# Linear attention and a gated feed-forward: another layout of pieces, tiles, banks and engines

## The chip, the cores and the metric

The kernel runs on one core of a Trainium2 chip. The metric is the device time of one execution in microseconds (us), as a median over runs. The engines are TensorE (PE; PEld is its weight load), VectorE (DVE), ScalarE (ACT) and GpSimd (POOL). SyncE (SP) issues most transfers; they run on the core's 16 DMA engines. Matmuls write to PSUM, which has eight banks, and DVE or ACT copies from there to SBUF.

## The reference

First an attention with a decaying state, per batch b (4) and head h (8), over 768 tokens with head size 48:

```
cur   = (u * k_t) outer v_t
y_t   = r_t . (state + cur)
state = w * state + k_t outer v_t
```

Then the heads are put side by side (x, 768 tokens of 384 channels) and go through a gated linear unit:

```
gate_pre[t] = sum over j of conv_w[j] * x[t - 4 + j]      (5 taps, causal, per channel)
out = (sigmoid(gate_pre) * (x @ w_val)) @ w_out
```

Inputs and outputs are float32; matmul operands are bf16 in both kernels.

## The kernel before

The sequence of each batch is cut in units of W = 256 tokens (12 in all, n = 0 to 11), and a unit in two chunks of 128 (cl, or c). The recurrence is computed by chunks. r and k are scaled by powers of w (dr, dk), transposed by products with an identity, and multiplied to scores; a triangular mask turns the scores into the attention inside a chunk (at); the state z carries what came before the chunk; the bonus u comes in through a row sum s and dv = s * v.

One unit passes through these steps (names in the order string, line of the profile in brackets):

- RS (L245) and KS (L274) scale r and k into rs and ks, on POOL, in some cases on DVE. RT (L259) and KT (L297) transpose them on PE into a bank, eight products of 128 columns each. RE (L267) and KE (L307) copy the banks to rT and kT on ACT. r is loaded with two neighbouring tokens in a partition, so RE undoes that order with a strided write.
- PR (L316) multiplies the transposed k with rT on DVE; S (L328) sums that with u * w on PE; SE (L340) copies the sums on DVE; DV (L343) makes dv on POOL. CV (L283) casts v to vb on ACT.
- A (L357) makes the scores in two banks per chunk, M (L370) masks a bank on DVE. KV (L384) makes the chunk's state on PE, ID (L396) adds the state before on DVE, in PSUM, and ZE (L401) multiplies it with a block mask or the decay, on DVE, to z.
- YD (L412) and Y (L426) gather the output of a chunk in one bank: 3 products with dv, 12 with z, 16 with at. Each of the latter fills a 128x32 tile of the array. YE (L455) copies the bank to xT on ACT.

The feed-forward works on the same 256 tokens. C (L470) is the convolution: per tap a diagonal 64x64 block times xT, 40 products of 256 columns for two thirds of the channels and 40 of 128 for the last third, whose tokens are split over two banks. SG (L483) is the sigmoid on ACT, V (L490, L499) the product with w_val, HT (L512) the product of both on DVE, O (L522) the product with w_out per chunk, OE (L534) the copy on ACT, and st (L538) stores a whole unit, 384 KB. The last unit is done by chunks of 128 (lines 560 to 640).

At the start w is loaded into all 128 partitions by a broadcast transfer (192 KB), its logarithm is taken (LN), and dr and dk follow as exponentials on ACT. Three products on the identity (D, L149) stand in the early PE stream.

There are no loops that set the order: a long string ORDER names every step, and each engine executes its steps in the order of the string. An engine's instruction that waits holds back all that stand behind it on this engine. That goes for SP's transfers too: nearly all loads and all stores but one are in one queue, loads first, and the 11 stores of whole units behind the last load:

```
v:11.1 ... st:4 ... st:0 ... st:1 ... st:2 ... st:7
```

PSUM tiles come from a pool of eight banks in turn; k_st and v_st have seven buffers, r_st six.

Of the kernel before, what the change touches and what calls it, by code (L numbers as in the profile page):

```python
# [12 lines left out]
AX = mybir.AxisListType  # L13
# [3 lines left out]
def kernel(  # L17
# [12 lines left out]
    nc = tc.nc  # L30

    B, H, S, D = r.shape
    C = 128
    NP = H // 2
# [4 lines left out]
    U = 2  # L39
    W = U * C  # L40
    NU = S // W
    N = B * NU

    consts = ctx.enter_context(tc.tile_pool(name="consts", bufs=1))
    persist = ctx.enter_context(tc.tile_pool(name="persist", bufs=1))
    ld = ctx.enter_context(tc.tile_pool(name="ld", bufs=7))
    ldr = ctx.enter_context(tc.tile_pool(name="ldr", bufs=6))
    wk = ctx.enter_context(tc.tile_pool(name="wk", bufs=2))
    atp = ctx.enter_context(tc.tile_pool(name="atp", bufs=4))
    ffn = ctx.enter_context(tc.tile_pool(name="ffn", bufs=2))  # L50
    outp = ctx.enter_context(tc.tile_pool(name="outp", bufs=11))

    psum = ctx.enter_context(tc.tile_pool(name="psum", bufs=8, space=bass.MemoryType.PSUM))

# [3 lines left out]
    def bank(shape=(128, 512), dtype=F32):  # L58
        return psum.tile(list(shape), dtype, name="bank")

    k_st, v_st, r_st = {}, {}, {}

    def load_kv(n, cl, nm, eng):
        b, cu = divmod(n, NU)
        src, d = (k, k_st) if nm == "k" else (v, v_st)
        if n not in d:
            d[n] = ld.tile([128, U, H, D], F32, name=f"{nm}_st")
        t0 = cu * W + cl * C
        eng.dma_start(out=d[n][:, cl], in_=src[b, :, t0 : t0 + C, :].transpose([1, 0, 2]))

    def load_r(n, eng, hs=(0, H)):
        b, cu = divmod(n, NU)
        if n not in r_st:
            r_st[n] = ldr.tile([128, H, 2, D], F32, name="r_st")
        hs = slice(*hs)
        eng.dma_start(
            out=r_st[n][:, hs].rearrange("p h s d -> p h (s d)"),
            in_=r[b, hs, cu * W : cu * W + W, :].rearrange("h (p s) d -> p h (s d)", s=2),
        )

    w_bc = consts.tile([128, H, D], F32)
    cw5 = consts.tile([KW, DM], F32)

    def load_w():
        nc.sync.dma_start(
            out=w_bc.rearrange("p h d -> p (h d)"),
            in_=w.rearrange("(o h) d -> o (h d)", o=1).to_broadcast([128, DM]),
        )

    def load_cw():  # L90
        nc.sync.dma_start(out=cw5, in_=moe_conv_w)

    ident = consts.tile([128, 128], BF16)
    make_identity(nc, ident)
    wt = consts.tile([128, NP], F32)
    nc.vector.memset(wt, 1.0)
    ut = consts.tile([128, NP], F32)
    nc.vector.memset(ut, 0.0)
    nc.scalar.preload_act_table_set("natural_log_exp_and_others")
    for dst, src in ((wt, w), (ut, u)):  # L100
        for par in range(2):
            nc.scalar.dma_start(
                out=dst[64 * par : 64 * par + D, :],
                in_=src.rearrange("(p two) d -> two d p", two=2)[par],
            )


    io_i32 = consts.tile([128, 1], mybir.dt.int32)
    nc.gpsimd.iota(io_i32, pattern=[[0, 1]], base=0, channel_multiplier=1)
    io_j = consts.tile([128, 2], mybir.dt.int32)  # L110
    nc.gpsimd.iota(io_j, pattern=[[1, 2]], base=0, channel_multiplier=2)
    mask = consts.tile([128, 128], BF16)
    make_upper_triangular(nc, mask, val=1.0, diag=False)

    io_f = consts.tile([128, 1], F32)
    nc.vector.tensor_copy(io_f, io_i32)
    sc_k = consts.tile([128, U], F32)
    for cl in range(U):
        nc.vector.tensor_scalar(
            sc_k[:, cl : cl + 1], io_f, scalar1=-1.0, scalar2=float(C - 1 - cl * C),  # L120
            op0=ALU.mult, op1=ALU.add,
        )
    sc_r = consts.tile([128, 2], F32)
    nc.vector.tensor_copy(sc_r, io_j)
    nc.vector.tensor_scalar_add(sc_r, sc_r, float(-C))

    lnw_bc = consts.tile([128, H, D], F32)
    dk = consts.tile([128, U, H, D], F32)
    dr = consts.tile([128, H, 2, D], F32)

    def log_w():
        nc.scalar.activation(out=lnw_bc, in_=w_bc, func=AF.Ln)

    def decay_r():
        for j in range(2):
            nc.scalar.activation(
                out=dr[:, :, j, :], in_=lnw_bc, func=AF.Exp, scale=sc_r[:, j : j + 1]
            )

    def decay_k():  # L140
        for cl in range(U):
            nc.scalar.activation(
                out=dk[:, cl], in_=lnw_bc, func=AF.Exp, scale=sc_k[:, cl : cl + 1]
            )

    def dummy():
        t_ = bank()
        for _ in range(3):
            nc.tensor.matmul(  # L149
                out=t_.rearrange("p (a x) -> p a x", x=128),  # L150
                lhsT=ident,
                rhs=ident[:, None, :].to_broadcast([128, 4, 128]),
                start=True,
                stop=True,
            )

    def ring(name, shape, n, dtype=BF16):
        return [persist.tile(shape, dtype, name=f"{name}{i}") for i in range(n)]

    def heads(t_, n):  # L160

        return t_[:, 16 : 16 + 64 * n].rearrange("p (h x) -> p h x", x=64)[:, :, 0:D]

    def gaps(t_):
        return t_.rearrange("p (h x) -> p h x", x=64)[:, :, 0:16]

    ks_t = ring("ks", [128, U, NP, 2, 64], 3)
    rs_t = ring("rs", [128, 2, NP, 2, 64], 2)
    vb_t = ring("vb", [128, U, H * 64 + 64], 4)
    dv_t = ring("dv", [128, U, DM], 2)  # L170
    xT_t = ring("xT", [128, NT, PAD + S], 2)
    for t_ in rs_t:
        nc.gpsimd.memset(t_[:, :, :, :, D:64].rearrange("p s n a x -> p (s n a) x"), 0.0)
    for t_ in ks_t:
        nc.gpsimd.memset(t_[:, :, :, :, D:64].rearrange("p c n a x -> p (c n a) x"), 0.0)
    for t_ in vb_t:
        nc.gpsimd.memset(gaps(t_.rearrange("p c x -> p (c x)")), 0.0)
    for t_ in xT_t:
        nc.gpsimd.memset(t_[:, :, 0:PAD], 0.0)

    uw2 = consts.tile([128, NP, 2], BF16)
    nc.gpsimd.memset(uw2, 0.0)
    wcm = consts.tile([128, NP, 2, D], F32)
    nc.gpsimd.memset(wcm, 0.0)
    bdm = consts.tile([128, NP, 2, D], F32)
    nc.gpsimd.memset(bdm, 0.0)
    for par in range(2):
        nc.gpsimd.memset(bdm[64 * par : 64 * par + 64, :, par, :], 1.0)

    wv_st = consts.tile([128, NT, DM], F32)
    wo_st = consts.tile([128, NT, DM], F32)

    wval = consts.tile([128, NT, 4, 128], BF16)
    wout = consts.tile([128, 4, DM], BF16)
    cw5b = consts.tile([KW, DM], BF16)
    cwT = consts.tile([128, NT, KW], F32)
    cwd = consts.tile([128, NT, KW, 64], BF16)
    id64 = consts.tile([128, 64], BF16)  # L200

    for q in range(2):
        rows = slice(64 * q, 64 * q + 64)
        nc.vector.tensor_copy(id64[rows], ident[rows, rows])

    def cw_cast():
        nc.vector.tensor_copy(cw5b, cw5)  # L207

    def cw_transp():
        st["cw_ps"] = bank([128, NT, 8], BF16)  # L210
        for T in range(NT):
            nc.tensor.transpose(
                st["cw_ps"][:, T, 0:KW], cw5b[:, T * 128 : T * 128 + 128], ident[0:KW, 0:KW]
            )

    def cw_evac():
        nc.vector.tensor_copy(cwT, st["cw_ps"][:, :, 0:KW])

    def cw_diag():
        nc.vector.tensor_tensor(  # L220
            out=cwd.rearrange("p t k x -> p (t k) x"),
            in0=id64[:, None, :].to_broadcast([128, NT * KW, 64]),
            in1=cwT.rearrange("p t k -> p (t k)")[:, :, None].to_broadcast([128, NT * KW, 64]),
            op=ALU.mult,
        )

    def cast_wval():
        wv = wv_st.rearrange("p k (t x) -> p k t x", x=128)
        nc.gpsimd.tensor_copy(wval[:, :, 0::2, :], wv[:, :, 0::2, :])
        nc.gpsimd.tensor_copy(wval[:, :, 1::2, 64:128], wv[:, :, 1:3, 0:64])  # L230
        nc.gpsimd.tensor_copy(wval[:, :, 1::2, 0:64], wv[:, :, 1:3, 64:128])

    def cast_wout(part):
        if part:
            nc.scalar.copy(out=wout[64:128, 1::2, :], in_=wo_st[0:64, 1:3, :])
            nc.scalar.copy(out=wout[0:64, 1::2, :], in_=wo_st[64:128, 1:3, :])
        else:
            nc.gpsimd.tensor_copy(wout[:, 0::2, :], wo_st[:, 0::2, :])


    st = {}

# [571 lines left out]
```

## Time and profile before

| quantity | value |
|---|---|
| median of 3 runs | 104.72 us (104.08 to 104.97) |
| span of the profiled execution | 102.6 us |
| instructions in it | 4615 |
| moved by DMA | 20.55 MB, 15.54 read from and 4.72 written to HBM |
| DMA packets | 67645, of which 63525 are under 512 B |
| mean granted TensorE clock | 0.944 (0.5 from some 17 to 27 us) |

The span is one execution, from the first to the last instruction on the core; the 2.1 us between it and the median lie around it. A line of the table of groups names a source line, engine, operation and tiles, the busy time, the mean duration and the idle time ahead of it. A line of a stretch gives for each engine its busy time in that stretch and the number of its instructions. The DMA share is the sum of the packets' times over 16 engines; as packets overlap, it can pass 1. Busy PE time is modelled from a pipelined engine, and isn't PE at its peak.

### The profile page before, as it was taken

What the parts mean: (1) busy time and instruction counts of PE and PEld (TensorE: products, weight loads), DVE (VectorE), ACT (ScalarE), POOL (GpSimd) and SP (SyncE); (2) the same over time, 40 slices, a digit from 0 to 9 for tenths busy, and PEclk for the clock granted to TensorE, in tenths of its full rate; (3) what the DMA queues carried; (4) which work ended last, traced back from release to release, by engine and by line L of the source; (5) the groups of instructions that cost most, each with busy time, mean ns of one, the idle gap of its engine ahead of it and who ended that gap; (6) DMA issues with size and microseconds to landing.
All of it is one profiled execution on the core that took longest, in us unless ns stands there. A gap on an engine that the chain in (4) does not pass through costs nothing.

```text
span 102.6 us, 4615 instructions
## 1 busy us (share of the span) xinstructions
PE 84.6 (82%) x2016; PEld 68.3 (67%) x2016; DVE 75.7 (74%) x148; ACT 72.8 (71%) x123; POOL 58.2 (57%) x63
## 2 busy tenths in 40 slices
PE   0002846999987999999899979999899999999980
PEld 0002435878766887898687648997698978887830
DVE  4004465886999998998789499999875986997230
ACT  5056555941988799977969967988798499835840
POOL 7951049799683706983995678738166990140000
PEclk9999996555899999999999999999999999999997
DMA  1799999999888799697979799879899897088673
GB/s 35 145 246 245 207 166 183 237 224 318 151 257 155 150 234 201 125 240 151 255 134 244 151 194 279 163 152 257 123 200 162 163 356 262 6 296 312 233 273 126
DMA packets 67645, 20.55 MB, mean 200 GB/s; under 512 B 63525, under 2 KB 67626, under 8 KB 67626
## 3 DMA queue, kind: packets, MB, share of 16 engines
q1 hardware_dynamic: 65610, 19.77, 86.8%
q10 hardware_dynamic: 2016, 0.49, 2.4%
q8 instruction: 15, 0.25, 1.0%
q14 instruction: 4, 0.03, 0.1%
HBM read 15.54 MB, written 4.72 MB: 198 GB/s over the span
## 4 chain that ended last, share of the span: by engine, by line
PE 51%; DMA 16%; DVE 13%; ACT 8%; issue 4%; POOL 3%; SPq 2%; DVEq 0%; POOLq 0%; ACTq 0%
PE bank L470 8%; PE bank L522 7%; PE bank L426 6%; DMA r_st<-in_r_dram 6%; DMA k_st<-in_k_dram 6%; PE bank L490 5%; DVE at L370 5%; DMA cw<-in_moe_conv_w_dram 5%; PE bank L297 5%; ACT kT L307 4%; PE bank L357 4%; PE bank L259 4%; PE bank L499 3%; PE bank L412 2%; PE bank L384 2%
## 5 line engine op out<-in xcount | busy, mean ns | idle before, releaser
L370 DVE TENSOR_TENSOR at<-bank,mask 128x512 bf16<-128x512 f32 x48 | 31.2, 681 | 3.3 <-PE bank L357 2.9
L343 POOL TENSOR_TENSOR dv<-v_st,s_sb 128x768 bf16<-128x768 f32 x12 | 17.7, 1475 | 12.5 <-DVE s_sb L340 10.9
L274 POOL TENSOR_TENSOR ks<-k_st,dk 128x768 bf16<-128x768 f32 x9 | 16.7, 1859 | 11.8 <-DVE cw5b L207 5.4
L307 ACT COPY kT<-bank 128x1024 bf16<-128x1024 bf16 (+1 forms) x13 | 12.4, 956 | 9.3 <-DVE pr L316 6.4
L267 ACT COPY rT<-bank 128x1024 bf16<-128x1024 bf16 (+1 forms) x13 | 16.1, 1237 | 2.5 <-PE bank L259 2.2
L259 PE MATMUL bank<-ident,rs 128*128 128x128 bf16 x96 | 8.4, 234 | 10.5 <-DVE rs L245 9.7
L245 POOL TENSOR_TENSOR rs<-r_st,dr 128x768 bf16<-128x768 f32 x8 | 14.5, 1818 | 3.0 <-DMA r_st<-in_r_dram 3.0
L522 PE MATMUL bank<-wout,hT 128*128 128x384 bf16 x66 | 14.2, 326 | 0.1
L259 PEld LDWEIGHTS <-rs 128*128 128x128 bf16 x96 | 6.3, 104 | 11.7 <-POOL uw L689 9.7
L455 ACT CAST xT<-bank 128x384 bf16<-128x384 f32 x24 | 10.7, 488 | 4.5 <-PE bank L426 4.4
L512 DVE TENSOR_TENSOR hT<-bank,gate 128x384 bf16<-128x384 f32 x22 | 11.6, 546 | 0.2 <-PE bank L522 0.2
L483 ACT ACTIVATE gate<-bank 128x384 bf16<-128x384 f32 x22 | 9.8, 500 | 2.6 <-PE bank L470 1.8
L470 PE MATMUL bank<-xT,cwd 64*64 64x128 bf16 (+1 forms) x440 | 11.2, 244 | 0.6 <-DVE at L370 0.3
L534 ACT COPY o_sb<-bank 128x384 f32<-128x384 f32 x22 | 10.3, 488 | 1.4 <-PE bank L522 0.9
L470 PEld LDWEIGHTS <-cwd 64*64 64x64 bf16 x440 | 9.7, 106 | 1.9 <-issue 0.8
L490 PE MATMUL bank<-xT,wval 128*128 128x256 bf16 x66 | 10.8, 272 | 0.0
L297 PE MATMUL bank<-ident,ks 128*128 128x128 bf16 x96 | 8.6, 239 | 2.4 <-DVE ks L274 1.4
L316 DVE TENSOR_TENSOR pr<-bank,rT 128x1024 bf16<-128x1024 bf16 (+1 forms) x13 | 8.3, 642 | 3.0 <-ACT kT L307 1.7
L283 ACT CAST vb<-v_st 128x768 bf16<-128x768 f32 x12 | 10.2, 852 | 0.0
L426 PE MATMUL bank<-at,vb 128*32 128x128 bf16 x384 | 9.8, 230 | 0.0
L357 PE MATMUL bank<-rT,kT 48*128 48x128 bf16 x192 | 8.8, 229 | 0.7 <-DVE bank L396 0.3
L297 PEld LDWEIGHTS <-ks 128*128 128x128 bf16 x96 | 6.6, 107 | 4.2 <-DVE ks L274 2.2
(79 smaller groups left out, 140.1 us busy)
## 6 DMA issues: line engine op xcount, KB each, us to landing
k_st<-in_k_dram SPq DMA_DIRECT2D x24, 192.0 KB, 5.4
v_st<-in_v_dram SPq DMA_DIRECT2D x24, 192.0 KB, 4.8
out_dram<-o_sb SPq DMA_DIRECT2D x11, 384.0 KB, 4.5
r_st<-in_r_dram SPq DMA_DIRECT2D x10, 384.0 KB, 5.4
wv_st<-in_moe_w_val_dram SPq DMA_DIRECT2D x1, 576.0 KB, 6.5
wo_st<-in_moe_w_out_dram SPq DMA_DIRECT2D x1, 576.0 KB, 6.3
r_st<-in_r_dram SPq DMA_DIRECT2D x2, 192.0 KB, 5.5
r_st<-in_r_dram ACTq DMA_DIRECT2D x1, 384.0 KB, 5.5
```

What stands on the lines that cost most here:

```text
L245: eng.tensor_tensor(out=rs_t[n % 2][:, :, ps[0] : ps[1], :, 0:D].rearrange("p s n a d -> p (n a) s d"), in0=r_st[n][:, hs], in1=dr[:, hs], ...
L259: nc.tensor.transpose(tr[:, s, p, :], rs_t[n % 2][:, s, ps[0] + p].rearrange("p a x -> p (a x)"), ident,)
L267: nc.scalar.copy(out=st["rT", n][:, ps[0] : ps[1], :].rearrange("x n (i s) -> x s n i", s=2), in_=st["r_tr", n, ps[0]],)
L274: eng.tensor_tensor(out=ks_t[n % 3][:, cs, :, :, 0:D].rearrange("p c n a d -> p c (n a) d"), in0=k_st[n][:, cs], in1=dk[:, cs], op=ALU.mult,)
L297: nc.tensor.transpose(tr[:, c, p, :], ks[:, cls[0] + c, p].rearrange("p a x -> p (a x)"), ident,)
L307: nc.scalar.copy(out=st["kT", n].rearrange("x n (c i) -> x c n i", c=U)[:, cls[0] : cls[1]], in_=tr,)
L343: eng.tensor_tensor(out=dv_t[n % 2].rearrange("p c (h d) -> p (c h) d", d=D), in0=v_st[n].rearrange("p c h d -> p (c h) d"), in1=st["s", n ...
L370: nc.vector.tensor_tensor(out=st["at", n, cl][:, par], in0=st["at_ps", n, cl][par], in1=mask[:, None, :].to_broadcast([128, NP, 128]), op= ...
L426: nc.tensor.matmul(out=y_ps[32 * q : 32 * q + 32, T, :], lhsT=lt, rhs=rh, start=False, stop=last, skip_group_check=True,)
L470: nc.tensor.matmul(out=g_ps[i][64 * qo : 64 * qo + 64, o0 : o0 + n0], lhsT=cwd[rows, T, t, :], rhs=xT[rows, T, t0 + c0 + t : t0 + c0 + t + ...
L490: nc.tensor.matmul(out=v_ps[:, 0:W], lhsT=wval[:, kt, i, :], rhs=xT[:, kt, t0 : t0 + W], start=(kt == 0), stop=(kt == NT - 1), skip_group_ ...
L522: nc.tensor.matmul(out=o_ps, lhsT=hT[:, i, c0 : c0 + C], rhs=wout[:, k, :], start=(j == 0), stop=(j == 2),)
```

## The change

The kernel is written anew, with the same mathematics, 12 units and two chunks. These parts differ:

- The feed-forward has pieces of its own: 384 tokens, half a batch, independent of the units. The last half is cut in 128 and 256.
- The convolution uses 32x32 diagonal blocks: 4 row strips times 3 channel groups, per tap 12 products that each have the whole piece's tokens as columns, and write to three banks. Group T lands rotated by T strips; columns of w_val and rows of w_out are rotated alike, w_out by its transfers (five of them).
- w is loaded as one row of 1.5 KB and spread to 128 partitions by a product with ones (WS, a float32 matmul).
- The copy of the transposed r reads the bank with a stride and writes rT densely; before, it read densely and wrote with a stride.
- The state before is added by a product with the identity on PE (ZI) instead of an addition on DVE (ID).
- PSUM is one tile of eight banks. Each step in ORDER names its bank (@) and, where there is a choice, its engine (/V, /A, /P for DVE, ACT, POOL). Of the 13 copies RE, 6 are on DVE (two of them halves); of the 13 KE, 4; of the 12 SE, 5. POOL has three whole casts of v and a half one, DVE one dv and one xT copy. DVE has one r product and one k product whole and a half of each (before, three whole r, two whole k and two halves of each); POOL has the others.
- No dummy product is named. Rings k_st and v_st have six buffers, the output ring has 12 of 128 tokens.
- A store is 128 tokens (192 KB), 24 in all. Three of them stand in SP's queue ahead of the last load of k, four more ahead of the last load of v.

The core of it, with the lines of the new order that hold the last loads:

```diff
-        for T0, t1, tn in ((0, 0, W), (2, 0, 0)):
-            for t in range(KW):
-                for q in range(2):
-                    for i in range(2):
-                        rows = slice(64 * q, 64 * q + 64)
-                        qo = (q + i) % 2
+    PIECES = (
+        (0, 0, 3), (0, 3, 3), (1, 0, 3), (1, 3, 3), (2, 0, 3), (2, 3, 3),
+        (3, 0, 3), (3, 3, 1), (3, 4, 2),
+    )
+    def conv(m, b):
+        bb, q0, nq = PIECES[m]
+        N, t0 = nq * C, q0 * C
+        for t in range(KW):
+            for q in range(4):
+                for T in range(NT):
+                    rows = slice(32 * q, 32 * q + 32)
+                    qo = (q + T) % 4
+                    nc.tensor.matmul(
+                        out=PS[32 * qo : 32 * qo + 32, b[T], 0:N],
+                        lhsT=cwd[rows, T, t, :],
+                        rhs=xT_t[bb % 2][rows, T, t0 + t : t0 + t + N],
...
-            in_=w.rearrange("(o h) d -> o (h d)", o=1).to_broadcast([128, DM]),
+        q.dma_start(out=wrow, in_=w.rearrange("(o h) d -> o (h d)", o=1))
+    def w_spread(b):
+        nc.tensor.matmul(out=bank(b, DM), lhsT=ones, rhs=wrow, start=True, stop=True)
...
-            out=st["rT", n][:, ps[0] : ps[1], :].rearrange("x n (i s) -> x s n i", s=2),
-            in_=st["r_tr", n, ps[0]],
+            rT_t[n % NRT][:, cut(half, NP)].rearrange("x n (p s) -> x n p s", s=2),
+            bank16(b)[:, cut(half, 1024)].rearrange("x (n s p) -> x n p s", s=2, p=128),
...
-        nc.vector.tensor_tensor(out=kv_ps, in0=kv_ps, in1=st["zin", n, cl], op=ALU.add)
+        nc.tensor.matmul(
+            out=bank(b, DM),
+            lhsT=ident,
+            rhs=z_t[2 * n % NZ].rearrange("p n a d -> p (n a d)"),
+            start=False,
...
+        st:1.1/S st:0.2/S v:11.1/S st:3.2/S O:5.1@0 st:1.2/S v:11.0/S st:3.1/S st:2.1/S st:2.0/S ZE:10.0@1
```

More of the change, by code (lines that the diff above doesn't have):

```diff
@@ L71, in load_r, with bank @@
[L71 to L77, printed above, removed]
+    psum = ctx.enter_context(tc.tile_pool(name="psum", bufs=1, space=bass.MemoryType.PSUM))
+    ctx.enter_context(tc.manual_schedule())
+    PS = psum.tile([128, 8, 512], F32, name="PS")
+    def bank(i, n=512):
+        return PS[:, i, 0:n]
@@ L109 @@
[L109 to L121, printed above, removed]
-        )
@@ L123 @@
[L123 to L137, printed above, removed]
-            )
@@ new lines, in bonus, with evac_s @@
+    def bonus(n, b):
+        for c in range(2):
+            for i in range(NP):
+                nc.tensor.matmul(
+                    out=bank(b)[:, c * H + 2 * i : c * H + 2 * i + 2],
+                    lhsT=pr_t[n % NPR][:, c, i, :],
+                    rhs=uw2[:, i, :],
+                    start=(c == 0 and i == 0),
+                    stop=(c == 1 and i == NP - 1),
+                    skip_group_check=True,
+                )
+    def evac_s(eng, n, b):
+        copy(eng, s_t[n % NDV].rearrange("p s h -> p (s h)"), bank(b, 2 * H))
@@ new lines, in attn @@
+    def attn(n, c, b):
+        rT, kT = rT_t[n % NRT], kT_t[n % NKT]
+        for i in range(NP):
+            for a in range(2):
+                rows = slice(64 * a, 64 * a + D)
+                nc.tensor.matmul(
+                    out=bank(b[a])[:, 128 * i : 128 * i + 128],
+                    lhsT=kT[rows, c, i, :],
+                    rhs=rT[rows, i, C * c : C * c + C],
+                    start=(i == 0),
+                    stop=(i == NP - 1),
+                    skip_group_check=True,
+                )
@@ L151, in dummy, with evac_o, store @@
+    def evac_o(eng, m, i, b):
+        copy(eng, o_t[o_index(m, i) % NO], bank(b, DM))
+    def store(m, i, q):
+        bb, q0, nq = PIECES[m]
+        t0 = (q0 + i) * C
+        q.dma_start(out=out[bb, t0 : t0 + C, :], in_=o_t[o_index(m, i) % NO])
+    def dummy(b):
+        for _ in range(2):
+            nc.tensor.matmul(
+                out=bank(b).rearrange("p (a x) -> p a x", x=128),
                 lhsT=ident,
@@ L171 @@
[L171 to L182, printed above, removed]
```

1046 lines of the change are left out of this document (464 added, 582 removed).

## The prediction

> **What bounds the kernel now.** I read the engines' shares first, then the stretches, then the queue of SP, and the chain of waits last.
>
> The first part of the page:
>
> ```profile
> PE 84.6 (82%) x2016; PEld 68.3 (67%) x2016; DVE 75.7 (74%) x148; ACT 72.8 (71%) x123; POOL 58.2 (57%) x63
> ```
>
> PE has most work, but no engine fills the span. The stretches (span time, length, then PE, PEld, DVE, ACT and POOL busy, the granted clock, the DMA share, GB/s):
>
> ```profile
> 0.00:16.00 16.00, 3.96 (x35) 2.51 (x35) 5.80 (x18) 7.83 (x13) 7.86 (x31) 1.00 0.94 174
> 16.00:36.00 20.00, 18.80 (x405) 15.45 (x409) 17.32 (x31) 13.75 (x20) 15.20 (x12) 0.74 0.97 210
> 36.00:60.00 24.00, 22.90 (x566) 18.61 (x555) 20.80 (x40) 21.54 (x38) 16.62 (x10) 1.00 0.97 193
> 60.00:80.00 20.00, 19.42 (x523) 16.48 (x522) 17.45 (x34) 15.65 (x27) 12.57 (x8) 1.00 0.97 189
> 80.00:92.00 12.00, 12.00 (x311) 10.02 (x313) 10.62 (x21) 9.16 (x16) 5.94 (x4) 1.00 0.70 223
> ```
>
> From 16 to 80 us two resources are full at once: PE (18.8 of 20, 22.9 of 24, 19.4 of 20) and the DMA engines, at 0.97 throughout. The rate is only 190 to 210 GB/s there; the page counts 63525 of 67645 packets under 512 B. The timeline of SP says the same (start, length, line, transfer):
>
> ```profile
> 0.75 0.43 SPq L69 DMA_DIRECT2D k_st<-in_k_dram  x1
> ...
> 49.13 3.33 SPq L69 DMA_DIRECT2D v_st<-in_v_dram  x2
> ...
> 76.14 0.71 SPq L69 DMA_DIRECT2D k_st<-in_k_dram  x1
> 76.89 2.94 SPq L69 DMA_DIRECT2D v_st<-in_v_dram  x2
> 80.33 17.84 SPq L538 DMA_DIRECT2D out_dram<-o_sb  x11
> ```
>
> An issue into an empty queue takes 0.43 us. The 49 issues from 16.72 to 79.83 take 61.0 of those 63 us, 1.2 each: SP is held up by the transfers ahead of it. The last k is issued at 76.14, and POOL's last key product starts on it at 81.21. After the last loads all stores follow, up to the end. The chain of waits (start, length, piece) is PE nearly alone from 74 us:
>
> ```profile
> 75.56 1.80 PE bank L470 x80
> ...
> 88.59 0.90 PE bank L426 x56
> ...
> 95.67 1.00 PE bank L560 x80
> ```
>
> So before, loads and PE run neck and neck to 80 us, and PE with a backlog sets the end. The execution profiled has a span of 102.6 us; the median of the runs is 104.72, so 2.1 us lie around the span, and I add them to each span below.
>
> **The change, part by part.** *Convolution on PE.* Now 80 products of a 256-token unit take 1.79 us (80 in 1.80 above): 11 units 19.7 us, the last one (L560) 1.0, together 20.7. They go away. Instead 540 products of 32x32 come in nine pieces of 60. No 32x32 product is in the trace. Low end: 12.5 ns each, as L560 goes (80 in 1.00); high end: no more side by side than the 64x64 ones, 15,360 columns in 1.79 us, so 23,040 columns of a 384-token piece take 2.7. I take the 128x32 products of L426, which are short and packed (56 in 0.90, 16 ns each): 0.96 a full piece, 0.75 for the two short ones, 8.2 in all. Bounds 6.8 and 21.5.
>
> The Trainium skill ("TensorE: Matmul & The Clock Gate", section "Measured speedup vs the span model") measured 6.32 times the speed of one tile for nine 32x32 tiles and 10.6 for sixteen. Twelve are in turn here; about 8 would be 1.2 us a piece, an estimate from that page, and the sum below would be 2 us larger. The rows for column tiles here (56 in 0.90, 3.3 side by side of four) are of the same kind.
>
> *Other PE work.* The carry moves from DVE into 8 identity products of 384 columns: 8 x 0.163 (three L522 take 0.49) = 1.3. The three dummies (1.5) go. Spreading w is one fp32 product of 384 columns; the trace has no fp32 product, so between 0.16 and four times a half-clock 0.33; I take 0.6. Values and projections have as many columns as before. PE: 84.6 - 20.7 - 1.5 + 8.2 + 1.3 + 0.6 = **72.5** (71 to 86).
>
> *DVE.* Off: four r and k products by shapes 2.8 + 2.0, the carry 8 x 0.558 = 4.5, half the diagonals 0.85, seven s copies 1.2. On: one dv 1.1, one xT copy 0.55, the memsets of vb (between 0.06 and 0.33 each) 0.8, small ones 0.1, four kT copies, and four and two halves of rT. A kT copy is dense bf16 from a bank, as pr (0.684) is: 2.7. The rT copy reads with a stride of 128 elements, not in the trace. Low end 0.68; high end the dearest rate of DVE, k's product (768 in 1.483), so 1.98. I take 1.2, the one-per-cycle rate of the mask rows (384 in 0.55, 512 in 0.68), as a stride spoils pairing at worst: 4 x 1.2 + 2 x 0.68 = 6.2. DVE: 75.7 - 11.35 + 11.45 = **75.8** (73 to 82): no relief.
>
> *ACT.* rT: 16.1 becomes 7 x 1.02 (the dense kT row; 1.33 if the strided side costs alike on the read) = 7.2; kT 12.4 becomes 8.3; casts of v 10.2 become 7.3; seven s copies +1.4; weights -0.8. 72.8 becomes **57.5** (up to 60). *POOL.* One and a half more k and two and a half more r products (1.86, 1.82) +7.4, casts of v +2.9, one dv -1.5, weights -1.8, memsets -1.2: 58.2 becomes **64**.
>
> *Transfers.* r, k, v and the output move the same bytes in the same packets. Only w's broadcast (192 KB) goes; w_out comes in five parts, stores in 24 of 192 KB, not 11 of 384. Six k and v buffers instead of seven cost nothing: a buffer's products are done some five units before its turn. The queue is full, so what is moved counts by place: three stores now stand ahead of the last k and four more ahead of the last v. A 192 KB store is 0.63 us at the 313 GB/s of the 92 to 96 us stretch, a 192 KB load 1.04 at 189. Each of these stores waits on SP for its copy by ACT, and every load behind it waits too; the three belong to the first two pieces, whose copies stand by the scores of units 4 and 5 in the order, and the loads behind them are of units 9 to 11, so I cost the wait at nothing (an ACT copy late by x moves the end by x). The last k: 81.2 - 0.6 (w) + 3 x 0.63 + 0.5 (an estimate for the start, where all of r goes by SP and none by ACT) = 83.0. The last v: + 4 x 0.63 + 2 x 1.04 = 87.6.
>
> *From there.* v cast 0.82, dv 1.48 (POOL): 89.9. y products 0.34 + 0.90, xT 0.55: 91.7. Convolution 0.75, three gates 1.2, hT 0.42, two projections 0.98, copy 0.49: 95.6. Store 1.9 to land, 1.0 to the end as before (issue 99.88, 1.7 to land, span 102.6): 98.5. By the queue alone, 17 stores after the last v: 87.6 + 10.7 + 1.0 = 99.3. The road over k (83.0, 1.82, transposes 0.45, copy and pr 1.4, scores 0.56, four masks 2.7) is at 89.9, no later. I take a span of 99.0: **101.1 us**. PE's 13 us mostly turn into waiting for loads: 10 units at 7.0 us of DMA against 6.0 of PE and 6.2 of DVE.
>
> **Rivals.** *Transfers go faster once fewer things stand beside them.* For: 260 GB/s from 20 to 24 us; against: 0.97 in every stretch, at rates that don't follow PE. Then DVE's 6.3 a unit sets the pace: the second unit's keys at 14, ten units 77, 16 us of tail and stores: 93 to 94, about **96 us**. *32x32 products run only as many at once as 64x64 ones.* PE is 86 again, starts some 1 us earlier, with its old idle 18: about 103, **105 us**, no change.
>
> *Slower: evacuation becomes the bound.* DVE keeps 75.8 us of work, now with strided copies between PE's products and the scores (RE and KE at L250). Its idle time, 102.6 - 75.7 = 26.9, need not shrink: if it is start, end and turns with PE, each us of DVE work is one of span. At strided copies near 1.7, halfway to the high end, DVE is 78; with k copies at 1.2, 80: 107 span, **108 us**. It decides above a DVE sum of about 77. For: DVE is full at 87% from 16 to 92 us. Against: among the waits PE's own for DVE are small after the start (the scores wait 0.3 us for it), while DVE waits 2.9 us for the scores. The Trainium skill ("TensorEngine Tiling (Array Packing)", section "PSUM Bottleneck") says this too: a tiled TensorE may leave the copies out of PSUM as the bottleneck. The trace agrees so far that PE waits little for them before.
>
> **How the numbers follow.** Forecast 0.48, faster transfers 0.13, no packing 0.13, evacuation 0.26. The first two lie below 103.7, the last above 105.8: faster by over 1% 0.61, within 1% (about what a measurement of this kernel can tell) 0.13, slower 0.26. The range runs from 97.5, inside the second case, to 107, inside the last, and leaves out some 0.2. The likeliest sign's own range is 98 to 103.7.
>
> **What would show it.** PE near 72 us busy with gaps in mid-kernel; a convolution piece near 0.96; DMA still at 0.95 or more up to some 85 us; SP's issues still over 1 us; the last k product near 83; ACT under 61, DVE near 76. Wrong if loads end well before 80 us, if DVE's sum passes 78, or if PE waits mostly for DVE and ACT rather than for products of loaded data.

## The result, and the profile after

The changed kernel took 98.70 us in the median of 6 runs (98.12 to 101.70); the kernel before took 104.30 beside it (6 runs, 103.33 to 104.97). The ratio is 0.947, with a 95% interval of 0.941 to 0.953. Some executions of one kernel take a few per cent longer than the rest: times here are medians of all runs, ratios are taken over the faster runs alone, and the execution whose profile is read (100.07 us, span 98.1, where most had spans of 96.2 to 96.8) is one of the longer.

The page of the changed kernel: the engines' shares, then the queue that SP and ACT fill, then the shares of the chain of waits.

```profile
PE 84.0 (86%) x1962; PEld 61.1 (62%) x1962; DVE 78.0 (80%) x145; ACT 59.0 (60%) x117; POOL 64.5 (66%) x69
...
q1 hardware_dynamic: 66748, 20.07, 85.2%
...
PE 50%; DVE 17%; POOL 12%; DMA 7%; issue 6%; ACT 3%; SPq 1%; POOLq 0%; DVEq 0%
```

ACT lost 13.8 us, POOL gained 6.3, DVE 2.3. PE's busy time hardly fell (84.6 before); its weight loads did (68.3 before). The queue's share, last in its line, is the time of all its packets over 16 engines: 85.2% of 98.1 us is 83.6 us an engine. Before, it was 86.8% of 102.6, 89.1 us, for nearly the same bytes.

The stretches of the changed kernel (span time, length, PE, PEld, DVE, ACT and POOL busy, granted clock, DMA share, GB/s):

```profile
0.00:16.00 16.00, 7.80 (x76) 5.82 (x77) 10.79 (x28) 8.99 (x14) 10.27 (x30) 1.00 0.93 195
16.00:36.00 20.00, 18.90 (x446) 13.70 (x445) 16.75 (x29) 12.14 (x23) 17.34 (x17) 1.00 0.95 221
36.00:60.00 24.00, 23.68 (x530) 16.91 (x525) 22.20 (x38) 15.77 (x33) 17.79 (x12) 1.00 0.98 211
60.00:80.00 20.00, 19.00 (x521) 14.35 (x520) 17.25 (x30) 13.84 (x28) 16.31 (x11) 1.00 0.90 212
80.00:92.00 12.00, 12.00 (x388) 8.85 (x387) 9.93 (x20) 5.61 (x16) 2.80 (x3) 1.00 0.64 226
```

The DMA engines are about as full as before, but move 195, 221, 211 and 212 GB/s where they moved 174, 210, 193 and 189. That is this execution: in another profile of the same kernel (the third group below) it was 217, 181 and 201 GB/s from 16 to 80 us, with the DMA engines at 0.93, 0.86 and 0.90. PE does 7.8 us of work in the first 16 us (3.96 before). As its busy time is only 0.6 us less in the whole, 3.9 of the 4.5 us that the span lost are idle time of PE, and nearly all of that lies before 16 us.

SP's timeline of the changed kernel (start, length, line, transfer), at its last loads:

```profile
72.33 2.09 SPq L268 DMA_DIRECT2D k_st<-in_k_dram  x2
74.53 1.52 SPq L538 DMA_DIRECT2D out_dram<-o  x2
76.15 0.40 SPq L268 DMA_DIRECT2D v_st<-in_v_dram  x1
76.64 1.11 SPq L538 DMA_DIRECT2D out_dram<-o  x2
77.81 0.46 SPq L268 DMA_DIRECT2D v_st<-in_v_dram  x1
78.32 17.24 SPq L538 DMA_DIRECT2D out_dram<-o  x17
```

The last k is issued at 73.72 and has landed at 77.2 (before: 76.14 and 80.9), although three stores now stand ahead of it. The last v has landed at 82.0 (before: 83.7), with seven stores ahead.

The chain of waits of the changed kernel (start, length, piece):

```profile
73.38 0.97 PE PS L482 x60
...
87.64 0.49 PE PS L524 x3
...
91.11 0.76 PE PS L482 x60
...
94.72 0.48 ACT o L248
```

From 70.7 us to 94.7 it is PE nearly alone: over 12 us of it after the last v has landed. A convolution piece takes 0.97 us.

The groups of the changed kernel, each shape apart (busy time, mean ns of one, idle time ahead of them):

```profile
L248 ACT COPY rT<-PS 128x1024 bf16<-128x1024 bf16 x7 | 7.1, 1014 | 2.3 <-PE PS L294 2.3
...
L250 DVE COPY rT<-PS 128x1024 bf16<-128x1024 bf16 x4 | 4.9, 1215 | 0.0
L250 DVE COPY kT<-PS 128x1024 bf16<-128x1024 bf16 x4 | 2.8, 689 | 0.4 <-PE PS L304 0.3
...
L166 PE MATMUL PS<-wrow,ones 1*128 1x384 f32 x2 | 1.6, 908 | 3.5 <-DMA wrow<-in_w_dram 3.5
```

The strided copy of rT takes 1215 ns on DVE and 1014 on ACT, where the dense kT copy takes 689 and 1013: the stride costs DVE a factor of 1.76, and ACT nothing.

**Where the loads' time went.** The loads of k and v come in packets of 192 bytes, those of r in packets of 384. The trace has 49,152 of the first in both kernels. In the kernel before they take 17.41 ns in the mean, in the changed one 15.41; most take 15 ns in both, and what differs is how many do: 80% are done within 16 ns before, 98.6% after. Spread over 16 engines that is 6.1 us. One thing about these transfers that differs is where their buffers lie on a partition. By the addresses in the built programs, all k_st, v_st and r_st begin 32 bytes past a multiple of 64 in the kernel before, and on multiples of 128 in the changed one. Nothing in the diff names that; it follows from the tiles declared ahead of them. What runs beside the transfers differs too, so the place is moved alone below.

### The profile page after: what moved, and what is told of

It is laid out like the page before. It is cut to its first block, busy times and chain, and to the rows that moved or that the text cites. A ratio compares the mean times of both kernels' runs of the same rounds, so it can differ in the third digit from the quotient of the medians.

```text
span 98.1 us, 4549 instructions
## 1 busy us (share of the span) xinstructions
PE 84.0 (86%) x1962; PEld 61.1 (62%) x1962; DVE 78.0 (80%) x145; ACT 59.0 (60%) x117; POOL 64.5 (66%) x69
## 3 DMA queue, kind: packets, MB, share of 16 engines
q1 hardware_dynamic: 66748, 20.07, 85.2%
## 4 chain that ended last, share of the span: by engine, by line
PE 50%; DVE 17%; POOL 12%; DMA 7%; issue 6%; ACT 3%; SPq 1%; POOLq 0%; DVEq 0%
PE PS L501 8%; PE PS L433 8%; PE PS L524 8%; DMA k_st<-in_k_dram 7%; DVE at L381 6%; PE PS L371 5%; PE PS L304 4%; PE PS L482 4%; PE PS L294 4%; POOL ks L283 4%; POOL rs L274 4%; PE PS L422 3%; POOL dv L350 3%; PE PS L393 3%; DVE pr L327 3%
## 5 line engine op out<-in xcount | busy, mean ns | idle before, releaser
L381 DVE TENSOR_TENSOR at<-PS,mask 128x512 bf16<-128x512 f32 x48 | 31.0, 683 | 2.8 <-PE PS L371 1.5
L283 POOL TENSOR_TENSOR ks<-k_st,dk 128x768 bf16<-128x768 f32 (+1 forms) x11 | 19.1, 1741 | 6.8 <-DMA k_st<-in_k_dram 5.8
L274 POOL TENSOR_TENSOR rs<-r_st,dr 128x768 bf16<-128x768 f32 (+1 forms) x11 | 19.4, 1771 | 5.9 <-DMA r_st<-in_r_dram 2.6
L248 ACT COPY o<-PS 128x384 f32<-128x384 f32 x24 | 11.3, 484 | 6.8 <-PE PS L524 6.7
L524 PE MATMUL PS<-wout,hT 128*128 128x384 bf16 x72 | 15.0, 326 | 0.0
L493 ACT ACTIVATE gate<-PS 128x384 bf16<-128x384 f32 (+2 forms) x27 | 10.7, 456 | 7.1 <-PE PS L482 5.7
L501 PE MATMUL PS<-xT,wval 128*128 128x384 bf16 (+2 forms) x81 | 14.6, 308 | 0.0
L248 ACT CAST xT<-PS 128x384 bf16<-128x384 f32 x23 | 10.6, 487 | 6.2 <-PE PS L433 6.0
L511 DVE TENSOR_TENSOR hT<-PS,gate 128x384 bf16<-128x384 f32 (+2 forms) x27 | 12.7, 505 | 1.8 <-ACT gate L493 0.9
L371 PE MATMUL PS<-rT,kT 48*128 48x128 bf16 x192 | 10.0, 240 | 0.8 <-DVE rT L250 0.4
L248 ACT COPY rT<-PS 128x1024 bf16<-128x1024 bf16 x7 | 7.1, 1014 | 2.3 <-PE PS L294 2.3
L524 PEld LDWEIGHTS <-hT 128*128 128x128 bf16 x72 | 6.2, 97 | 3.5 <-issue 0.2
```

The source lines that it names most:

```text
L248: eng.copy(out=dst, in_=src)
L274: eng.tensor_tensor(out=rs_t[n % NRS][:, :, ns, :, 0:D].rearrange("p s n a d -> p (n a) s d"), in0=r_st[n % NRL][:, hs], in1=dr[:, hs], op ...
L283: eng.tensor_tensor(out=ks_t[n % NKS][:, cs, :, :, 0:D].rearrange("p c n a d -> p c (n a) d"), in0=k_st[n % NLD][:, cs], in1=dk[:, cs], op ...
L371: nc.tensor.matmul(out=bank(b[a])[:, 128 * i : 128 * i + 128], lhsT=kT[rows, c, i, :], rhs=rT[rows, i, C * c : C * c + C], start=(i == 0), ...
L381: nc.vector.tensor_tensor(out=at_t[n % NAT][:, c, a], in0=bank(b).rearrange("p (n x) -> p n x", x=128), in1=mask[:, None, :].to_broadcast( ...
L501: nc.tensor.matmul(out=bank(b, N), lhsT=wval[:, kt, T, :], rhs=xT_t[bb % 2][:, kt, t0 : t0 + N], start=(kt == 0), stop=(kt == NT - 1),)
```

## Experiments

Twelve kernels were run, in three groups of four, each group on one chip beside the kernel before. The kernel before took 104.92, 105.37 and 104.98 us in them, and the changed kernel itself, run unaltered in the third, came to 0.958 of it and not 0.947. So variants are compared within a group wherever the group allows it.

### Where the landing buffers lie

In the changed kernel 32 bytes of padding (8 columns), in one variant 64 (16 columns) and in one 96 (24), go ahead of the landing buffers, and a second padding tile behind them brings what follows to a place with its old remainder within 64 bytes:

```diff
+    pad0 = consts.tile([128, 8], F32, name="pad0")
     r_st = ring("r_st", [128, H, 2, D], NRL, F32)
...
     v_st = ring("v_st", [128, 2, H, D], NLD, F32)
+    pad1 = consts.tile([128, 8], F32, name="pad1")
```

In the kernel before, one such tile of 32 bytes stands ahead of the persistent buffers; all that lies behind it moves along, the output tiles too. The first two of these runs:

> The changed kernel with 32 bytes of padding ahead of r_st and 32 more behind v_st, so that only the landing buffers of r, k and v move: they start at 32 bytes past a multiple of 64, as in the kernel before, instead of on a multiple. Background: in the changed kernel a 192-byte packet took 15.4 ns on average, before 17.4, and the last k landed at 77.2 us, before at 80.9. Theory 1 (the place of the landing buffers makes the difference): mean 192-byte packet 17 or more, last k at 80 or later, time 100.5 to 102. Theory 2 (packets are slower where something else runs beside them, the place is nothing): packets stay at 15.4, time 98.7 within 0.7.

> The kernel before with 32 bytes of padding at the end of the pool ahead of the landing buffers, which then start on a multiple of 64; the pools behind it move along. Theory 1 (place): 192-byte packets near 15.4 ns, last k near 77, and time 102 to 103.5, as PE's backlog keeps part of the gain from the end. Theory 2 (place is nothing): packets stay at 17.4, time 104.3 within 0.7.

The shifted changed kernel took 106.61 us in the median: one run of 102.42 (0.976 of before), three of 106.56 to 106.92. Its packets took 17.52 ns, and the last k landed at 86.3. The shifted kernel before took 103.08 us, 0.981 of the unshifted (0.973 to 0.988), its packets 16.11 ns, and 91% of them were done within 16 ns. So the place sets the length of the packets, in both directions, and the time goes the way of Theory 1. Not all of that theory held: in the kernel before the last k landed at 79.4, not near 77, and the last v at 83.8, no sooner than without padding (83.7). The unaltered changed kernel did not run in this group, so the shift was repeated by other amounts beside it:

> The changed kernel unaltered, beside its variants on one chip, as the measure for them. Every theory: 0.945 to 0.96 of the kernel before, 192-byte packets at 15.4 to 15.6 ns.

> The changed kernel with 64 bytes of padding before the landing buffers of r, k and v, so that they move but stay on a multiple of 64 (from 128 to 192 past a multiple of 512). Theory R (what counts is the remainder within 64 bytes): packets stay at 15.4 to 15.6 ns and the time within 1% of the unaltered kernel beside it. Theory D (any other place than the one the written order was made with costs, whatever its remainder): 192-byte packets above 16.5 ns and 102 us or more.

> The same with 96 bytes of padding: the landing buffers begin 32 bytes past a multiple of 64 again, at another place than in the first shift (there 106.6 us and 17.5 ns). Theory R: packets at 17 to 18 ns, last k load landed after 83 us, 102 to 107 us. A rival, that the first shift was slow for another reason than its remainder: as the unaltered kernel, 98 to 101 us and 15.4 to 15.6 ns.

> The changed kernel with three padding tiles, so that the landing buffers of r, k and v and the output tiles begin on multiples of 512 bytes (they begin at 128 and 320 past one) and the two expert weights' landing buffers on multiples of 256 (they begin at 32 past a multiple of 64). If only the place within 64 bytes counts for the loads: 192-byte packets stay at 15.4 ns, only the weights' 1536-byte packets may gain, 98 to 99 us. If every larger alignment helps: packets under 15 ns and 96 to 97.5 us.

The last of these was run in the group of the kernels without v loads and with later stores, below. Its edit is three padding tiles of 96, 80 and 56 columns:

```diff
+    pad0 = consts.tile([128, 96], F32, name="pad0")
     r_st = ring("r_st", [128, H, 2, D], NRL, F32)
...
+    pad2 = consts.tile([128, 80], F32, name="pad2")
     o_t = ring("o", [128, DM], NO, F32)
...
+    pad1 = consts.tile([128, 56], F32, name="pad1")
     wv_st = consts.tile([128, NT, DM], F32, name="wv_st")
```

All runs on this, by the place of the buffers (prompt: share of the 192-byte packets done within 16 ns):

| kernel | buffers begin | 192-byte packet | prompt | time | over before |
|---|---|---|---|---|---|
| before | 32 past a multiple of 64 | 17.41 ns | 80% | 104.30 | 1 |
| before, padded | 64 past a multiple of 128 | 16.11 | 91% | 103.08 | 0.981 |
| changed | multiple of 128 | 15.41 | 99% | 98.70 | 0.947 |
| changed, third group | multiple of 128 | 15.62 | 99% | 102.01 | 0.958 (0.949 to 0.967) |
| + 64 bytes | 64 past a multiple of 128 | 15.95 | 92% | 101.92 | 0.972 (0.964 to 0.980) |
| + 96 bytes | 32 past a multiple of 64 | 17.68 | 78% | 105.04 | 0.984 (0.978 to 0.991) |
| + 32 bytes | 32 past a multiple of 64 | 17.52 | 79% | 106.61 | 0.976 (one run) |
| larger multiples | multiple of 512 | 15.64 | 99% | 101.64 | 0.961 (0.948 to 0.975) |

The same is to be read from the page alone. The unaltered changed kernel in the third group, its span and its queue:

```profile
span 101.1 us, 4549 instructions
...
q1 hardware_dynamic: 66748, 20.07, 83.1%
```

The page of the kernel with 96 bytes of padding:

```profile
span 102.8 us, 4549 instructions
...
q1 hardware_dynamic: 66748, 20.07, 90.0%
```

The same packets and bytes need 84.0 us of the 16 engines in the one and 92.5 in the other. Theory R holds where it speaks of 32 bytes, and D falls: the kernel moved by 64 bytes keeps short packets. But R in its simple form misses that this kernel lies between (15.95 ns, 92%, and a ratio 1.4% above the unaltered one, the intervals just overlapping). There are three grades, not two, and 512 is no better than 128 (15.64 ns; its time, 0.961, is no better either, where 98 to 99 us were expected). That the kernel before with padding got only part of the way (16.11 ns) fits: its buffers came to rest 64 past a multiple of 128.

What the place is worth: between the 96-byte shift and the unaltered kernel 0.984 over 0.958, **2.8%**, the intervals apart; in the kernel before 1.9%, with 1.3 of the 2.0 ns. When the loads land follows the packets less closely. In the third group the last k landed at 83.1 us in the unaltered kernel, at 82.8 with 64 bytes and at 84.8 with 96. So the unaltered kernel can have short packets and still get its last k later than the kernel before (80.9).

### TensorE's work, or the loads

In the kernel before, two of the five convolution taps are left (the output lacks three), once alone and once with the 32 bytes of padding:

```diff
-            for t in range(KW):
+            for t in (0, KW - 1):
```

> The kernel before with only the first and last of the five taps computed (the other three are left out), so that its convolution costs 0.72 us a unit instead of 1.79, near the 0.65 of the changed kernel; PE loses some 12.4 us, all else stays. Theory P: 92 to 96. Theory L: the last loads land at 82 to 84 as before, some 15 us follow, 99.5 to 102.

> The kernel before with both single changes at once: two of the five convolution taps (the output leaves three taps out; TensorE has some 12.4 us less to do) and the landing buffers moved by 32 bytes onto multiples of 64. Alone they gave -2.6% and -1.9%. Theory J (TensorE and the loads bound it together, each hiding the other's gain): together they give clearly more than the sum of both, 97 to 99.5 us, and the last k load lands near 76 to 78 us. Theory S (the two act at different places and simply add): 100 us, between 99.7 and 100.7.

The 1.79, the 0.72 and the 12.4 us in these texts, like the 20.7 us of the prediction, are twice too large. They take a piece of 80 products in the chain for one unit. The program has 40 products a unit, 20 of 256 columns and 20 of 128, and the page of the kernel before has 440 of them for eleven units:

```profile
L470 PE MATMUL bank<-xT,cwd 64*64 64x128 bf16 (+1 forms) x440 | 11.2, 244 | 0.6 <-DVE at L370 0.3
```

Where the convolutions of two units follow each other on PE (C:7 and C:8 in the order), the chain joins them in one piece of 80. A unit's convolution that stands alone is shown with 40 products, and with 16 where two taps are left. First the chain of the kernel before, then that of the kernel with two taps:

```profile
84.25 0.95 PE bank L470 x40
```

```profile
89.16 0.45 PE bank L470 x16
```

So the convolution before cost some 11.5 us (eleven times 0.95, and 1.0 for the last unit), and the two taps take some 6 us from TensorE. Theory P's 92 to 96 us rested on 12.4; with 6 it would be some 98.

Two taps alone took 102.51 us, 0.974 (0.964 to 0.985): of some 6 us of TensorE's work 2.7 came through. The last loads landed a little sooner (k at 79.5, v at 81.5). The stretches of this kernel, 36 to 80 us:

```profile
36.00:60.00 24.00, 21.79 (x477) 17.41 (x470) 20.80 (x41) 21.32 (x35) 18.40 (x11) 1.00 0.98 194
60.00:80.00 20.00, 18.70 (x478) 15.55 (x472) 17.81 (x34) 15.73 (x28) 12.71 (x9) 1.00 0.97 186
```

The DMA share stays at 0.97 and 0.98 and the rate at 194 and 186 GB/s, as before with five taps. With the padding too it was 101.05 us, 0.960 (0.950 to 0.970). The two gains, 2.6% and 1.9%, come to 4.5 by their sum and 4.0 as measured. Theory S, plain addition, is nearer than J, which expected more than the sum, though the last k did land as J had it, at 76.7 us.

In the changed kernel TensorE gets more to do, in two ways: each piece of the convolution computed twice, or its blocks back at 64x64, the rows of the weights turned to match:

```diff
-        for t in range(KW):
+        for again in range(2):
+            for t in range(KW):
```

```diff
-            for q in range(4):
+            for q in range(2):
                 for T in range(NT):
-                    rows = slice(32 * q, 32 * q + 32)
-                    qo = (q + T) % 4
+                    rows = slice(64 * q, 64 * q + 64)
+                    qo = (q + T) % 2
...
-        m = 32 * T
+        m = 64 * (T % 2)
```

> The changed kernel with each convolution piece computed twice, the second time over the first, so that PE has 540 more 32x32 products, some 8.8 us, and its convolution costs about what it cost before (17.6 against 20.7). Theory P (PE's work sets the time, and the packed convolution is the gain): 105 to 108. Theory L (the loads set the pace, as forecast, and PE has 1 us of slack a unit): 99 to 101.5.

> One part undone: the convolution of the changed kernel goes back to 64x64 blocks (30 products a piece of 384 tokens where there were 60 of 32x32, each over a four times larger block; weights' rows turned to match). By the kernel before's work this is some 13 us more on TensorE. Theory P (TensorE's work in its written order decides in the changed kernel): 110 to 116 us, slower than the kernel before. Theory L (the loads set the pace, and the convolution's gain turned into waiting): 100 to 104 us.

Here too the 20.7 and the 13 us count the convolution before twice. Twice: 113.02 us, 1.076 of before (1.068 to 1.083). 64x64: 104.67 us, 0.989 (0.983 to 0.995), 3.2% over the unaltered kernel beside it. The chain of the 64x64 kernel:

```profile
67.14 1.80 PE PS L482 x30
...
86.94 1.75 PE PS L482 x26
```

A full piece takes 1.78 us or so, where 60 products of 32x32 take 0.97, and the short ones 0.69 and 1.22: 14.3 us for all nine instead of 8.2. Of these 6.1 us more, 3.2% of the time, some 3.2 us, came through, where Theory P would have all of it and Theory L next to nothing. This is not the convolution of the kernel before, which cost 11.5. In the variant the first and the third group of channels (T = 0 and 2) fall on the same 64x64 places of the array, as qo is the same for both, so that such a place gets 3,840 columns a piece. Before, the third group's tokens were split over two places, and each place got 1,920 columns a unit. The times fit: 1.80 us for 3,840, and 1.80 for two units of 1,920. The chain of the kernel that computes each piece twice:

```profile
70.40 1.09 issue
...
80.46 1.23 issue
...
90.98 1.78 PE PS L483 x117
...
96.70 1.79 issue
```

Its pieces take 1.78 us as well (1.12 and 1.32 the short ones), 6.7 us more for all nine. But five stretches of "issue", 5.9 us in sum, stand on PE, in which it waits for nothing that the profile shows; the changed kernel has one, of 0.72 us. Together that is 11.8 of the 13.8 us by which its span grew (98.1 to 111.9). So this kernel is no clean measure of TensorE's work. What the gaps are is not tested, but the trace has a hint. The page has a queue of the kind "instruction", with packets of 16 KB: 15 in the changed kernel, 13 in the one with 64x64 blocks, 19 here, in step with PE's 1962, 1692 and 2502 products and as many weight loads. Each of the five gaps ends 1.3 to 1.5 us after such a packet has ended (the three shown after those that ended at 69.98, 80.40 and 97.00), and the one in the changed kernel 1.5 us after. It looks as if PE ran out of instructions there.

Then the loads are relieved. In one kernel the twelve v loads of units 6 to 11 are left out:

```diff
-        v:7.1/S v:7.0/S V:1.0@2 WO:.2/A G:1.2@0 A:4.0@70 G:1.0@4 G:1.1@3 V:1.1@4 O:0.1@6 M:4.1@0 CV:3/A
+        V:1.0@2 WO:.2/A G:1.2@0 A:4.0@70 G:1.0@4 G:1.1@3 V:1.1@4 O:0.1@6 M:4.1@0 CV:3/A
...
-        st:1.1/S st:0.2/S v:11.1/S st:3.2/S O:5.1@0 st:1.2/S v:11.0/S st:3.1/S st:2.1/S st:2.0/S ZE:10.0@1
+        st:1.1/S st:0.2/S st:3.2/S O:5.1@0 st:1.2/S st:3.1/S st:2.1/S st:2.0/S ZE:10.0@1
```

> The changed kernel without the twelve v loads of units 6 to 11 (older v data stand in; the output is another one): some 12 us of transfers less, TensorE's work unchanged. Theory L (the loads still set the pace of the changed kernel, as my prediction had it): 93 to 96 us. Theory P (in the changed kernel the chain has gone over to TensorE's work; from 61 us to 95 us it is TensorE almost alone): 97 to 99 us, within 1.5% of the changed kernel's 98.7.

In the other seven stores are moved (the two lines that `st:0.1` and `st:1.0` leave are not shown):

```diff
-        ZE:7.0@0 M:7.2@7 r:11/S st:0.0/S v:10.0/S v:10.1/S M:8.0@3 DV:7/P YD:7.0@6 SE:8@1/A YI:7.0@6
+        ZE:7.0@0 M:7.2@7 r:11/S v:10.0/S v:10.1/S M:8.0@3 DV:7/P YD:7.0@6 SE:8@1/A YI:7.0@6
...
-        st:1.1/S st:0.2/S v:11.1/S st:3.2/S O:5.1@0 st:1.2/S v:11.0/S st:3.1/S st:2.1/S st:2.0/S ZE:10.0@1
+        v:11.1/S O:5.1@0 v:11.0/S st:0.1/S st:1.0/S st:0.0/S st:1.1/S
+        st:0.2/S st:3.2/S st:1.2/S st:3.1/S st:2.1/S st:2.0/S ZE:10.0@1
```

> The changed kernel with seven early output stores (0.63 us each, some 4.4 us of transfers) moved in the written order behind the last v load. Theory L (loads set the pace): the last k and v loads land some 3 to 4 us sooner, 96.5 to 98 us. Theory P (TensorE's work sets it): loads land sooner all the same, and the time stays within 1% of 98.7, or rises to 100 as the stores gather at the end.

Because buffers of the output ring are written again in the meantime, some of the moved stores carry a later piece's rows, so this kernel's output is another one too; work and bytes are the same.

Without the v loads it took 99.67 us, 0.947 of before (0.936 to 0.957). SP's timeline of that kernel:

```profile
61.91 2.23 SPq L268 DMA_DIRECT2D k_st<-in_k_dram  x2
64.23 29.81 SPq L538 DMA_DIRECT2D out_dram<-o  x21
```

and its stretches from 60 us on:

```profile
60.00:80.00 20.00, 19.68 (x547) 15.03 (x545) 18.23 (x33) 13.68 (x28) 16.82 (x12) 1.00 0.53 150
80.00:92.00 12.00, 12.00 (x369) 8.54 (x358) 9.49 (x20) 6.34 (x17) 1.48 (x1) 1.00 0.42 152
```

The last k has landed at 68.1 us, 9 us sooner than in the changed kernel; the DMA share falls to half; and the span, 96.7, is that of most executions of the changed kernel (96.2 to 96.8). With later stores it took 101.24 us, 0.964 (0.956 to 0.971); the last k landed at 77.5 and the last v at 79.5, where the kernel with larger alignment beside it had 81.9 and 85.3 and took 101.64. That kernel stands in for the unaltered one, which did not run in this group. Loads that land 4 to 6 us sooner bring no gain that can be told (0.964 beside 0.961), and 12 us of transfers less bring some 1.5% at most (0.947 beside 0.961, the intervals overlapping). So Theory P holds here: with loads as quick as these, TensorE's own order of work sets the end. None of the variants that do the whole work beat the changed kernel.

## Why the prediction was right, and where it was not

The sign was right, and the time within the range: 101.1 forecast, 98.70 measured, a ratio of 0.947 where I had 0.965 (101.1 over 104.72). The way to it was not. The gain on TensorE was put at nearly four times what it was, and the largest single part of the gain, the place of the buffers, was not foreseen. That the number came out near is in good part luck. Point by point:

- **"A full piece 0.96, the short ones 0.75":** 0.97 and 0.63 to 0.76. Sixty products of 384 columns one after the other would be 9.8 us at the 0.163 of the L524 products, so some ten run side by side. The estimate from the Trainium skill ("TensorE: Matmul & The Clock Gate", section "Measured speedup vs the span model"), 1.2 us a piece, was too high here. The rival of products that don't pack falls.
- **"80 products of a 256-token unit take 1.79 us" and "together 20.7":** a step that failed. The 80 products are two units' (the description of the kernel before has the same slip: 40 and 40 products where a unit has 20 and 20). The convolution went from some 11.5 us to 8.2, not from 20.7. The page's own rows would have shown it: 440 products, 11.2 us busy before, and now

```profile
L482 PE MATMUL PS<-xT,cwd 32*32 32x384 bf16 (+2 forms) x540 | 8.8, 306 | 0.0
```

- **"PE 72.5, with gaps in mid-kernel":** the page says 84.0, in full slices. With 11.5 for 20.7 the same sum gives 81.7, and 1.0 of the rest is the product that spreads w. The sign was a good one, and it failed because the saving was not there.
- **"PE's 13 us mostly turn into waiting for loads":** there were no 13 us, but some 3. PE is busy 73.6 of the 76 us from 16 to 92. By the corrected sum a unit takes 6.8 us of PE against the 7.0 of DMA, so the two limits were closer than the prediction had them. Of some 6 us more or less on TensorE about half comes through, in the kernel before (2.7 us) as in the changed one (3.2).
- **"DVE 75.8, ACT 57.5, POOL 64":** 78.0, 59.0 and 64.5. The rT copy was 1.21 for 1.2, the kT copy 0.69 for 0.68. Too low were the one dv on DVE (2.35 for 1.1; 0.96 in the third group's profile), the diagonals (1.44 for 0.85), and the fp32 product, which shows as two products of 0.9 us (1.6 together, for 0.6).
- **"It decides above a DVE sum of about 77":** the sum passed that point and nothing followed. Among PE's waits in the changed kernel, DVE is named for more than 0.5 us only once, at the start, though DVE's share of the chain rose from 13% to 17%. The rival is refuted, and with it, for this kernel, the Trainium skill's remark ("TensorEngine Tiling (Array Packing)", section "PSUM Bottleneck") that the copies out of PSUM may become the bound.
- **"r, k, v and the output move the same bytes in the same packets", and so at the same rate:** a step that failed as well. Bytes and packets are the same, the length of a packet is not: 17.4 to 17.7 ns against 15.4 to 15.6 by the place of the buffers, and 2.8% of the time with it. I listed faster transfers as a rival at 0.13, for another reason, less work beside them. I put the last k at 83.0 and the last v at 87.6; in the result's profile they landed at 77.2 and 82.0, with the DMA share at 0.90 from 60 to 80 us where I had 0.95.
- **"From there", and the queue, to 99.0:** in the result's profile this is not the road that decides. By it the kernel would have ended near 93; PE still had a backlog of over 12 us after the last v landed, ended at 94.7, and copy and store bring the span to 98.1. There 99.0 came out near because two errors met: the loads were put 5.6 us too late, and PE's work too small.

What the parts are worth: with its buffers back at the old remainder the changed kernel is at 0.984 of the kernel before (0.978 to 0.991), with them on multiples of 128 at 0.958. So of the 4.2% on that chip 2.8 hang on the place of the buffers, and all the rest of the change together is worth 1.6%. The convolution's 3.3 us would be some 1.5% of it, if half comes through as in the two trials (an estimate from them). What PE's earlier start, ZI, the searched order and the change of engines add or cost was not tried by itself; with the old remainder PE still did 7.0 us of work in the first 16 us, so the start is within that 1.6%, unless another part costs something. In the kernel before, padding alone gave 1.9%, two taps alone 2.6%, both 4.0%.

One thing stays open. With the same code the changed kernel's gain was 5.3% in the result and 4.2% in the third group (the intervals overlap between 0.949 and 0.953), and there the chain of its page reads differently, with the queue of SP ahead of PE:

```profile
SPq 40%; PE 26%; DMA 19%; POOL 5%; issue 3%; DVE 2%; ACT 2%; DVEq 0%; POOLq 0%; ACTq 0%
```

The chain of that profile takes the road of the prediction, over the last k:

```profile
77.67 5.39 DMA k_st<-in_k_dram
...
83.20 1.82 POOL ks L283
```

The last k landed at 83.1, where 83.0 was forecast, the v cast waits for the last v until 87.75, and from 85.1 us PE runs nearly alone to 97.7; the span is 101.1.

So which of the two limits is last can change from one chip or execution to the next, and why is not known; packets were hardly longer (15.62 ns).

The granted clock is not the cause of the gain, though the kernel before ran at half clock from some 17 to 27 us in its profile and the changed one did not: in the first group the kernel before took 104.92 and 105.79 us in its two runs at a mean clock of 1.0, and 104.75 to 105.80 in those at 0.95 to 0.97.

## What to carry to other kernels

Where many small packets fill the DMA engines, "the same bytes in the same packets" is not yet the same rate: before costing transfers by the old rate, look where the landing buffers come to lie, since any tile declared ahead of them moves them. Before you price a step by a piece of the chain, count the piece's products against the program and the page's row: a piece can join two steps, and a forecast gain of 13 us was 3. Where two limits stand close together, expect part of a relief to come through (here about half), and ask whether the change moves the other limit too.

## What the runs showed of the hardware

- Packets of 192 bytes into buffers that begin 32 bytes past a multiple of 64 take 17.4 to 17.7 ns in the mean (78 to 80% prompt), 64 past a multiple of 128 15.9 to 16.1 (91 to 93%), on a multiple of 128 or 512 15.4 to 15.6 (99%). For packets of 384 bytes the grades lie closer and overlap: 24.0 to 24.6 ns on multiples of 128, 24.5 to 25.0 at 64 past, 24.8 (the kernel before) to 26.7 at 32 past.
- The Trainium skill ("DMA: Bandwidth & Descriptors", section "How a descriptor splits into AXI transactions") says that a descriptor that doesn't begin on 256 bytes pays for the bytes before it, in beats of 32. It speaks of reads; here the bytes are written. Rows of 192-byte pieces come to 9 beats each in the mean from a multiple of 64 and 10 from 32 past one, an estimate by that page: 11% more, where the runs show 13%. The page would make 64 and 128 alike, and there the runs differ (15.95 and 15.62), so it isn't the whole of it.
- A copy out of PSUM that reads with a stride costs DVE 1.76 times the dense one (1215 for 689 ns), and ACT nothing (1014 for 1013).
- Products of 64x64 blocks on the same place of the array took 1.80 us for 3,840 columns in both kernels that have them; 60 products of 32x32 on twelve places, 1,920 columns each, took 0.97.
- TensorE showed five "issue" gaps of 0.7 to 1.8 us with 540 more small products, each ending 1.3 to 1.5 us after a 16 KB packet of the instruction queue; the cause is not tested.
